# The last matrix of the second layer's weights, converted from float64 beside the attention in memory of its own

## The chip, the cores and the metric

The kernel runs on one core of a Trainium2 chip. The metric is the device time of one execution in microseconds (us). A core has TensorE (PE, matrix products), VectorE (DVE), ScalarE (ACT), GpSimd (POOL) and SyncE (SP, which here issues nearly all loads and stores). Each engine has a queue of its own and works through it in order: an instruction that waits holds back everything behind it on that engine.

## The reference

Three blocks follow each other: an attention over a window of 128 keys, a layer of eight experts of which each token takes one, and a second layer of three products under a maximum. The weights of the second layer are float64 in memory, the others float32.

```python
# q, k, v: [4, 8, 576, 64] float32
scores = np.matmul(q, k.transpose(0, 1, 3, 2)) / 8           # plus a slope for distance, window 128
attn = softmax(scores);  x = (attn @ v) as [2304, 512]
...
logits = x @ w_gate + modality_bias[modality_id]             # 8 experts
h = np.maximum(x[mask] @ w1[e], 0.0)                         # 512 -> 1024, expert e for its tokens
x[mask] = gate_w[mask, None] * (h @ w2[e])                   # 1024 -> 512
...
h = np.maximum(np.maximum(x @ w1, x @ w2), x @ w3)           # float64, 512 -> 768
out = (h @ w_out).astype(np.float32)                         # float64, 768 -> 512
```

## The kernel before

Every product is made from float16 pieces: each operand is split into a high and a low float16 part, and three products (high by high, high by low, low by high) are added in float32. `PASSES` is that list.

**Order of the work.** The text of the program sets the order on every engine; nothing is reordered. Attention runs in steps of one group of four heads (`Attention.run`). When the first half of the tokens has its routes, the experts' layer of that half (`layer1(0)`, `layer1(1)`) is written between the steps of the attention, so that the two share the engines until the attention ends. What is left of `layer1(1)` then runs alone, then the second layer of the first half (`layer2(0)`), then both layers of the second half (`layer1(2)`, `layer1(3)`, `layer2(1)`).

**The experts' weights** (`Weights`). A piece of 512 KB is loaded into one of three staging tiles `st`, ScalarE writes its high part (L960), VectorE its low part (L969), both into one of four tiles `wt`. `get(n)` runs the high part three pieces ahead and issues loads five pieces ahead.

**The second layer's weights** (`Weights2`). There are 24 matrices of 512 KB: 18 of the three products (`g`, three for each of six blocks m) and six of `w_out` (`wo`). A matrix is loaded into a staging tile `st2` (four of them) and turned into float32 by three integer instructions on VectorE (L1113, L1117, L1122), which write a tile `b64` (five of them). `tick()` puts one of the three into the program. Then `finish()` has ScalarE scale it in place (L1142) and write the high part (L1143), and GpSimd writes the low part (L1144). `settled()` calls `finish()` for a matrix once `AGE` = 2 more ticks have gone by; `tick()` does nothing, and does not count, while too many matrices stand unfinished:

```python
if self.gen is None and (self.done == self.n or len(self.half) > B64 - 2):
    return
self.age += 1
```

**Where the ticks come from.** `layer1` adds up an estimate of TensorE time in `free` after each piece of work and calls `tick()` once for each `TICK` = 0.9 of it, but only once the attention has ended, since the tiles `st2`, `b64`, `g` and `wo` lie in a pool (`m2`) that takes the attention's memory. In `layer2(0)` `inner` calls two or four ticks before each product. `g` goes in the order of its use, `wo` comes last and is needed by `outer` (L1202), which first calls `convert(w.n)`.

Of the kernel before, what the change touches and what calls it, by code (L numbers as in the profile page):

```python
# [40 lines left out]
TICK = 0.9  # L41
# [3 lines left out]
ST2 = 4  # L45
B64 = 5
# [4 lines left out]
def windowed_attention_moe_kernel(  # L51
# [869 lines left out]
    class Weights:  # L921
# [10 lines left out]
        def issue(self, upto):  # L932
            while self.issued < min(upto, self.n):
# [6 lines left out]
                if self.more and self.issued % 7 in (1, 2, 4, 6):  # L940
                    st = self.more.tile([128, 1024], I32, name="st2", tag="st2", bufs=ST2).bitcast(F32)
                else:
                    st = self.pool.tile([128, 1024], F32, name="st", tag="st", bufs=3)
# [31 lines left out]
        def get(self, n):  # L975
            self.low(n + 2)
            self.high(n + 3)
            self.issue(n + (9 if self.more else 5))
# [73 lines left out]
    class Weights2:  # L1052
# [3 lines left out]
        def __init__(self, pool):  # L1056
            self.g = None
            self.wo = pool.tile([128, 2, K2, DM], F16, name="wo", bufs=1)
            self.pool = pool
            self.st = {}  # L1060
            self.n = 4 * K2
# [3 lines left out]

        def issue(self, upto):
            while self.issued < min(upto, self.n):
                n = self.issued
                st = self.pool.tile([128, 1024], I32, name="st2", tag="st2", bufs=ST2)
# [12 lines left out]
                self.st[n] = st  # L1082
                self.issued += 1

        def begin(self):
            g = self.pool.tile([128, 6 * K2 * KD * 128], F16, name="g", tag="g", bufs=1)
            self.g = g.rearrange("p (l i m k c) -> p l i m k c", l=2, i=3, m=K2, k=KD)
# [7 lines left out]
        def tick(self):  # L1095

            if self.gen is None and (self.done == self.n or len(self.half) > B64 - 2):
# [6 lines left out]
        def bits(self):  # L1104
# [7 lines left out]
            b = self.pool.tile([128, 512], I32, name="b64", tag="b64", bufs=B64)  # L1112
# [7 lines left out]
            self.issue(n + ST2)  # L1120
# [12 lines left out]
        def finish(self):  # L1133
            if not self.half:
                return
            n, b, _ = self.half.pop(0)
            if n < 3 * K2:
                m, i = divmod(n, 3)
                dst = [self.g[:, l, i, m].rearrange("p k c -> p (k c)") for l in range(2)]
            else:  # L1140
                dst = [self.wo[:, l, n - 3 * K2] for l in range(2)]
# [6 lines left out]
    def moe2(pool, items, w, hmt, n2=C2, both=False, **kw):  # L1148
# [24 lines left out]
        def inner(*xs):  # L1173
            for m in range(K2):
                w.convert(3 * m + 3)
                run = {}
                for i in range(3):
                    for x in xs:
                        for _ in range(4 if w.done < 3 * (m + 2) else 2):
# [13 lines left out]
        def outer(x, yT, c, idxs, gates):  # L1193
            w.convert(w.n)
            hm = hms[:, x % 2]
            for u in range(n2 // 128):
# [3 lines left out]
                for f in range(K2):  # L1200
                    for wl, xl in PASSES:
                        nc.tensor.matmul(  # L1202
                            out=ps, lhsT=hm[:, xl, f, 128 * u:128 * u + 128],
                            rhs=w.wo[:, wl, f, :], start=(n == 0), stop=(n == 3 * K2 - 1),
# [111 lines left out]
    with tc.manual_schedule():  # L1316
# [30 lines left out]
        yT = [big.tile([128, 2, KD, WY], F16, name="yT0", bufs=1)]  # L1347
        xa_cm = tc.tile_pool(name="xa", bufs=1)
# [4 lines left out]
        bats, w2s, m2 = [], None, None  # L1353
# [15 lines left out]
        def settle():  # L1369

            nonlocal w2s, m2, xh
# [3 lines left out]
            w2s = Weights2(m2)  # L1375
# [45 lines left out]
        def layer1(u):  # L1421
            nonlocal acc, free
            i = 0
            for c, dv in moe(mw, wst, u, xT[u], yT[u // 2], wait):
# [15 lines left out]
                if w2s:  # L1440
                    if not w2s.g:
                        w2s.begin()
# [78 lines left out]
```

## Time and profile before

| | us |
|---|---|
| median of 3 runs | 693.69 |
| lowest and highest run | 693.31 and 697.92 |
| the profiled execution, its own time | 690.42 |
| its span (first to last instruction) | 688.6 |
| TensorE busy / VectorE / ScalarE / GpSimd | 642.8 / 364.4 / 347.0 / 225.2 |

Times in the rows below are counted from the span's start. In names the buffer's number is left out, so that `st` stands for the experts' staging tiles and for the second layer's `st2`, and `b` for `b64`; `in_moe_w_dram` stands for the weights of both layers. A matmul's end is modelled, so that the number of matmuls in a stretch says more than TensorE's busy time.

### The profile page before, as it was taken

What the parts mean: (1) busy time and instruction counts of PE and PEld (TensorE: products, weight loads), DVE (VectorE), ACT (ScalarE), POOL (GpSimd) and SP (SyncE); (2) the same over time, 40 slices, a digit from 0 to 9 for tenths busy, and PEclk for the clock granted to TensorE, in tenths of its full rate; (3) what the DMA queues carried; (4) which work ended last, traced back from release to release, by engine and by line L of the source; (5) the groups of instructions that cost most, each with busy time, mean ns of one, the idle gap of its engine ahead of it and who ended that gap; (6) DMA issues with size and microseconds to landing.
All of it is one profiled execution on the core that took longest, in us unless ns stands there. A gap on an engine that the chain in (4) does not pass through costs nothing.

```text
span 688.6 us, 12881 instructions
## 1 busy us (share of the span) xinstructions
PE 642.8 (93%) x4787; PEld 399.7 (58%) x4787; DVE 364.4 (53%) x1083; ACT 347.0 (50%) x660; POOL 225.2 (33%) x232
## 2 busy tenths in 40 slices
PE   6899889989989997899899999999999999999993
PEld 5687755666657545755564564444448666656641
DVE  5977875865567599999922223152224455201100
ACT  5898887887757365854423211454647211111110
POOL 2111226343112255756534212472424111121121
PEclk9999999999999999999999999999999999999997
DMA  9655773455312665674323403343330000000011
GB/s 192 109 124 134 192 202 82 119 148 152 96 47 66 206 202 163 210 245 161 106 60 82 93 17 123 122 141 104 100 115 2 1 0 1 1 32 17 1 46 49
DMA packets 120800, 69.95 MB, mean 102 GB/s; under 512 B 68872, under 2 KB 115484, under 8 KB 120732
## 3 DMA queue, kind: packets, MB, share of 16 engines
q1 hardware_dynamic: 116992, 59.06, 32.2%
q0 software_dynamic: 3040, 9.96, 4.5%
q8 instruction: 40, 0.66, 0.4%
q14 instruction: 28, 0.23, 0.1%
q10 hardware_dynamic: 700, 0.04, 0.1%
HBM read 57.19 MB, written 9.44 MB: 97 GB/s over the span
## 4 chain that ended last, share of the span: by engine, by line
PE 70%; DVE 15%; ACT 8%; issue 3%; DMA 2%; POOL 1%; POOLq 0%; DVEq 0%; ACTq 0%; SPq 0%
PE m L1159 28%; PE m L1018 10%; PE m L997 10%; PE m L1202 9%; PE s L338 3%; PE m L471 2%; DVE wt L969 2%; PE m L379 2%; PE m L286 2%; ACT e L360 2%; DVE b L1117 2%; DVE e L351 2%; DVE b L1113 2%; PE bank L409 2%; ACT eh L385 1%
## 5 line engine op out<-in xcount | busy, mean ns | idle before, releaser
L1159 PEld LDWEIGHTS <-g 128*128 128x128 f16 x1296 | 126.7, 98 | 87.6 <-issue 4.3
L1159 PE MATMUL m<-yT,g 128*128 128x384 f16 x648 | 106.8, 326 | 2.5 <-DVE hx L1168 1.5
L969 DVE SCALAR_TENSOR_TENSOR wt<-st,wt 128x1024 f16<-128x1024 f32 x48 | 64.3, 1341 | 79.3 <-ACT wt L960 79.3
L1159 PE MATMUL m<-yh,g 128*128 128x384 f16 x648 | 105.7, 327 | 0.0
L1018 PE MATMUL m<-ht,wt 128*128 128x496 f16 (+3 forms) x576 | 102.3, 334 | 3.0 <-DVE wt L969 3.0
L1168 DVE SCALAR_TENSOR_TENSOR hx<-m,hx 128x384 f32<-128x384 f32 x72 | 39.7, 555 | 123.5 <-PE m L1159 120.9
L997 PEld LDWEIGHTS <-wt 128*128 128x128 f16 x576 | 55.8, 100 | 49.8 <-DVE wt L969 4.9
L989 POOL TENSOR_TENSOR ht<-hf,ht 128x496 f16<-128x496 f32 (+3 forms) x48 | 51.0, 1068 | 88.5 <-ACT ht L988 82.8
L1018 PEld LDWEIGHTS <-wt 128*128 128x128 f16 x576 | 54.1, 98 | 43.1 <-DVE wt L969 3.7
L360 ACT ACTIVATE e<-e,nm 128x256 f32<-128x256 f32 (+2 forms) x144 | 59.2, 471 | 27.4 <-DVE nm L351 27.0
L987 ACT ACTIVATE hf<-m 128x496 f32<-128x496 f32 (+3 forms) x72 | 35.9, 498 | 64.7 <-PE m L1018 31.9
L997 PE MATMUL m<-xT,wt 128*128 128x496 f16 (+2 forms) x288 | 59.5, 353 | 6.0 <-DVE wt L969 3.9
L997 PE MATMUL m<-xh,wt 128*128 128x496 f16 (+1 forms) x288 | 51.2, 330 | 0.0
L351 DVE CUSTOM_DVE_ANT_0 e<-s,bias 128x256 f32<-128x256 f32 (+1 forms) x128 | 45.8, 381 | 10.1 <-ACT e L360 4.8
L960 ACT ACTIVATE wt<-st 128x1024 f16<-128x1024 f32 x48 | 49.9, 1044 | 1.0 <-DMA st<-in_moe_w_dram 0.9
L390 DVE TENSOR_TENSOR el<-m,eh 128x512 f16<-128x512 f32 x64 | 42.2, 681 | 9.6 <-ACT eh L385 9.6
L1188 POOL TENSOR_TENSOR xh<-hx,xh 128x384 f16<-128x384 f32 x18 | 16.5, 914 | 89.8 <-ACT xh L1187 89.8
L338 PE MATMUL s<-kT,qT 64*128 64x256 f32 (+2 forms) x320 | 42.4, 386 | 3.3 <-DVE nm L351 2.2
L1187 ACT ACTIVATE xh<-hx 128x384 f16<-128x384 f32 x18 | 9.4, 523 | 71.1 <-DVE hx L1168 67.1
L314 POOL TENSOR_TENSOR vl<-rawv,vh 128x512 f16<-128x512 f32 (+1 forms) x20 | 22.5, 1125 | 65.2 <-ACT vh L307 65.2
L1208 ACT ACTIVATE ob<-m,gate 128x512 f32<-128x512 f32 x18 | 12.4, 687 | 55.0 <-PE m L1202 49.6
L385 ACT ACTIVATE eh<-m 128x512 f16<-128x512 f32 x64 | 34.7, 586 | 4.9 <-PE m L379 4.7
(184 smaller groups left out, 987.4 us busy)
## 6 DMA issues: line engine op xcount, KB each, us to landing
st<-in_moe_w_dram SPq DMA_DIRECT2D x66, 512.0 KB, 3.9
rawk<-in_k_dram SPq DMA_DIRECT2D x16, 256.0 KB, 4.3
rawq<-in_q_dram SPq DMA_DIRECT2D x16, 256.0 KB, 4.8
rawv<-in_v_dram SPq DMA_DIRECT2D x16, 256.0 KB, 4.0
xs<-x SPq DMA_DIRECT2D x16, 256.0 KB, 2.2
st<-in_moe_w_out_dram SPq DMA_DIRECT2D x6, 512.0 KB, 3.4
rawk<-in_k_dram SPq DMA_DIRECT2D x4, 128.0 KB, 5.5
rawq<-in_q_dram SPq DMA_DIRECT2D x4, 128.0 KB, 3.7
```

The source lines that it names most:

```text
L338: nc.tensor.matmul(out=out[u][rows, x // 2, c0:c1], lhsT=self.qT[b, t][r, i, 0:n], rhs=self.kT[b][r, i, k0 + c0:k0 + c1], start=True, stop ...
L351: nc.vector.tensor_tensor_reduce(out=e[:, x, c0:c1], in0=s[x % 2][:, x // 2, c0:c1], in1=bias[:, x, c0:c1], scale=-0.125, scalar=3.0e38, o ...
L360: nc.scalar.activation(out=e[:, x, c0:c1], in_=e[:, x, c0:c1], func=ACTF.Exp, scale=-1.0, bias=nm[:, x:x + 1],)
L385: nc.scalar.activation(out=b, in_=a, func=ACTF.Copy)
L390: nc.vector.tensor_tensor(out=o, in0=a, in1=b, op=ALU.subtract)
L960: nc.scalar.activation(out=wt[:, 0], in_=st, func=ACTF.Copy, scale=SW)
L969: nc.vector.scalar_tensor_tensor(out=wt[:, 1], in0=st.rearrange("p (a b) -> p a b", a=a), scalar=SW, in1=wt[:, 0], op0=ALU.mult, op1=ALU.s ...
L989: nc.gpsimd.tensor_tensor(out=lo, in0=hf, in1=hi[1], op=ALU.subtract)
L997: nc.tensor.matmul(out=ps, lhsT=wt[:, wl, kk, o:o + 128], rhs=xT[:, xl, kk, bass.ds(d[0], cap)], start=(n == 0), stop=(n == 3 * KD - 1),)
L1018: nc.tensor.matmul(out=ps, lhsT=wt[:, wl, f, :], rhs=hs[f][:, xl], start=(n == 0), stop=(n == 3 * KF - 1),)
L1159: nc.tensor.matmul(out=ps, lhsT=w.g[:, wl, i, m, kk, :], rhs=yT[:, xl, kk, c:c + n2], start=(n == 0), stop=(n == 3 * KD - 1),)
L1202: nc.tensor.matmul(out=ps, lhsT=hm[:, xl, f, 128 * u:128 * u + 128], rhs=w.wo[:, wl, f, :], start=(n == 0), stop=(n == 3 * K2 - 1),)
```

## The change

`Weights2` is made before the attention ends and gets a pool of its own (`wp`) for the six tiles of `wo`, for two staging tiles `st2` and for two tiles `b64`. The list `order` puts the six matrices of `w_out` first (`EARLY` = 6), then the 18 of `g`. During the attention `layer1` issues loads and ticks for these six, at `SHARE` = 0.3 of the rate. Once the attention has ended, `begin` opens rings of three `st2m` and three `b64m` in `m2` for the 18 others. `tick()` now returns while an unfinished matrix stands in `half` (during the attention), or while two do (after it). `issue(EARLY + ST2)` is called once the attention has ended. The staging tiles of the experts' weights of the second half change too (every second one in `st2m`, eight pieces ahead).

```diff
-ST2 = 4
-B64 = 5
+ST2 = 3
+EARLY = 6
+SHARE = 0.3
...
-                if self.more and self.issued % 7 in (1, 2, 4, 6):
-                    st = self.more.tile([128, 1024], I32, name="st2", tag="st2", bufs=ST2).bitcast(F32)
+                if self.more and self.issued % 2:
+                    st = self.more.tile([128, 1024], I32, name="st2m", tag="st2m", bufs=ST2).bitcast(F32)
...
-            self.issue(n + (9 if self.more else 5))
+            self.issue(n + (8 if self.more else 5))
...
-            self.g = None
-            self.wo = pool.tile([128, 2, K2, DM], F16, name="wo", bufs=1)
+            self.g = self.more = None
+            self.wo = [pool.tile([128, 2, DM], F16, name=f"wo{f}", bufs=1) for f in range(K2)]
...
+            self.order = [3 * K2 + f for f in range(EARLY)] + list(range(3 * K2))
+            self.order += [3 * K2 + f for f in range(EARLY, K2)]
...
+        def ring(self, x, nm, width):
+            if x < EARLY:
+                return self.pool.tile([128, width], I32, name=nm, tag=nm, bufs=2)
+            return self.more.tile([128, width], I32, name=nm + "m", tag=nm + "m", bufs=ST2)
+
         def issue(self, upto):
-            while self.issued < min(upto, self.n):
-                n = self.issued
-                st = self.pool.tile([128, 1024], I32, name="st2", tag="st2", bufs=ST2)
+            while self.issued < min(upto, self.n if self.more else EARLY):
+                n = self.order[self.issued]
+                st = self.ring(self.issued, "st2", 1024)
...
-            if self.gen is None and (self.done == self.n or len(self.half) > B64 - 2):
+            left = (self.n if self.more else EARLY) - self.done
+            if self.gen is None and (not left or len(self.half) > (1 if self.more else 0)):
                 return
...
-            b = self.pool.tile([128, 512], I32, name="b64", tag="b64", bufs=B64)
+            b = self.ring(n, "b64", 512)
...
-            self.issue(n + ST2)
+            self.issue(n + (ST2 if n >= EARLY else 2))
...
-                w.convert(3 * m + 3)
+                w.convert(EARLY + 3 * m + 3)
...
-                        for _ in range(4 if w.done < 3 * (m + 2) else 2):
+                        for _ in range(4 if w.done < EARLY + 3 * (m + 2) else 2):
...
+        wp = ctx.enter_context(tc.tile_pool(name="wp", bufs=1))
+        w2s = Weights2(wp)
...
-                if w2s:
-                    if not w2s.g:
-                        w2s.begin()
-                    w2s.issue(ST2)
-                    if w2s.done == w2s.n:
-                        wst.more = m2
-                    free += c - dv
-                    w2s.settled()
-                    while free > TICK:
-                        free -= TICK
-                        w2s.tick()
+                if m2 and not w2s.more:
+                    w2s.begin(m2)
+                w2s.issue(EARLY + ST2 if m2 else 2)
+                if w2s.done == w2s.n:
+                    wst.more = m2
+                free += (c - dv) * (1.0 if m2 else SHARE)
+                w2s.settled()
+                while free > TICK:
+                    free -= TICK
+                    w2s.tick()
```

Three places show what moves. The first is VectorE's queue just after the attention, at the first two matrices that are converted there; `r_` and `slot_` are routing of the second half, `wt` an expert's piece. Before:

```order
L1122 SCALAR_TENSOR_TENSOR b64_3996<-st2_3976,b64_3996 128x512
L1113 TENSOR_SCALAR b64_4026<-st2_3978 128x512 [waits DMAHW0_49]
L701 TENSOR_SCALAR r_pi_4014<-r_pi_4014 128x5
L702 TENSOR_SCALAR r_pi_4014<-r_pi_4014 128x5
L756 TENSOR_REDUCE r_mn2_3685<-r_le2_3684 1x1 [waits DVE_49]
L705 CAST r_pq_4042<-r_pi_4014 128x2x5 [waits DVE_49]
L758 SCALAR_TENSOR_TENSOR r_sd2_3682<-r_sd2_3682,r_mn2_3685 1x1 [waits DVE_49]
L710 TENSOR_TENSOR r_op_4045<-iota_r_78,r_pq_4042 128x640 [waits DVE_49]
```

After:

```order
L1134 SCALAR_TENSOR_TENSOR b64_4006<-st2_1941,b64_4006 128x512
L1125 TENSOR_SCALAR b64_4051<-st2_3992 128x512 [waits DMAHW1_49,Pool_49]
L702 TENSOR_SCALAR r_pi_4036<-r_pi_4036 128x5
L703 TENSOR_SCALAR r_pi_4036<-r_pi_4036 128x5
L757 TENSOR_REDUCE r_mn2_3702<-r_le2_3701 1x1 [waits DVE_49]
L706 CAST r_pq_4067<-r_pi_4036 128x2x5 [waits DVE_49]
L759 SCALAR_TENSOR_TENSOR r_sd2_3699<-r_sd2_3699,r_mn2_3702 1x1 [waits DVE_49]
L711 TENSOR_TENSOR r_op_4070<-iota_r_78,r_pq_4067 128x640 [waits DVE_49]
```

The matrix that starts here has a wait for GpSimd (Pool) that it didn't have: its tile `b64` is that of the matrix two before it, and GpSimd reads that last.

The second is SyncE's queue at the same time; `st2` and `st2m` are loads of the second layer's matrices, `st` those of the experts. Before:

```order
L1073 DMA st2_3978<-in_moe2_w2_dram 128x4x256 [waits DMAHW0_49]
L1073 DMA st2_3980<-in_moe2_w3_dram 128x4x256
L1073 DMA st2_3982<-in_moe2_w1_dram 128x4x256 [waits DMAHW2_49]
L951 ISA
L951 DMA st_3987<-in_moe_w2_dram 128x8x128 [waits DVE_49]
```

After:

```order
L1089 DMA st2_3994<-in_moe2_w_out_dram 128x1024 [waits DMAHW2_49,DVE_49]
L1089 DMA st2_3996<-in_moe2_w_out_dram 128x1024 [waits DMAHW3_49,DMAHW1_49,DVE_49]
L1089 DMA st2_3998<-in_moe2_w_out_dram 128x1024 [waits DMAHW4_49,DMAHW2_49,DVE_49]
L1083 DMA st2m_4000<-in_moe2_w1_dram 128x4x256 [waits DMASW5_49,DMASW6_49,DMASW4_49,DMASW7_49,DMASW1_49,DMAHW5_49,DMASW0_49,DMAHW6_49,PE_49,DMAHW7_49,Activation_49,Pool_49]
L1083 DMA st2m_4002<-in_moe2_w2_dram 128x4x256
L1083 DMA st2m_4004<-in_moe2_w3_dram 128x4x256
L952 ISA
L952 DMA st_4011<-in_moe_w2_dram 128x8x128 [waits DMAHW0_49]
```

The expert's piece (`st_3987`, now `st_4011`) stands behind three loads that wait for VectorE, each for the last of the three instructions on the matrix two before it.

The third is ScalarE's queue at the pieces and matrices that follow. Before:

```order
L1142 ACTIVATE b64_4026<-b64_4026 128x512 [waits DVE_49]
L1143 ACTIVATE g_3975<-b64_4026 128x512 [waits Activation_49]
L960 ACTIVATE wt_4121<-st_3987 128x1024 [waits DMAHW3_49]
L987 ACTIVATE hf_4159<-m_4125 128x480 [waits PE_49,Pool_49]
L988 ISA
L988 ACTIVATE yT0_749<-hf_4159 128x480 [waits Activation_49]
L1142 ACTIVATE b64_4096<-b64_4096 128x512 [waits DVE_49]
L1143 ACTIVATE g_3975<-b64_4096 128x512 [waits Activation_49]
```

After:

```order
L1155 ACTIVATE b64_4051<-b64_4051 128x512 [waits DVE_49,Pool_49]
L1156 ACTIVATE wo2_755<-b64_4051 128x512 [waits Activation_49]
L961 ACTIVATE wt_4143<-st_4011 128x1024 [waits DMAHW0_49]
L1155 ACTIVATE b64_4113<-b64_4113 128x512 [waits DVE_49,Pool_49]
L1156 ACTIVATE wo3_756<-b64_4113 128x512 [waits Activation_49]
```

The finishing of `b64_4113`, the fourth matrix of `w_out`, now stands directly behind the expert's piece that waits for its load.

## Rows read from the trace of the kernel before

**Rows 1.** Busy time of each engine in two stretches (columns PE, PEld, DVE, ACT, POOL, clock, DMA)

```profile
233.00:342.00 109.00, 99.54 (x655) 61.38 (x654) 104.22 (x169) 65.25 (x115) 64.63 (x53) 0.97 0.62 194
340.00:360.00 20.00, 20.00 (x125) 12.03 (x123) 8.54 (x12) 5.88 (x13) 8.37 (x8) 1.00 0.20 52
```

**Rows 2.** Chain that ended last, by line, from 222 to 300 us

```profile
by line: DVE wt L969 17.0%; DVE b L1117 10.1%; issue 9.7%; DVE b L1122 7.8%; DVE b L1113 7.8%; PE m L1159 6.5%; PE m L1018 5.9%; PE m L997 4.9%; DMA st<-in_moe_w_dram 4.7%; PE m L471 3.3%; DVE r_op L710 2.0%; DVE r_pq L705 1.6%; DVE r_le L7
```

**Rows 3.** Groups on VectorE from 236 to 343 us (count, then busy us, mean ns, idle before)

```profile
L1117 DVE SCALAR_TENSOR_TENSOR b<-st,b 128x512 int32<-128x512 int32 x24 | 25.8, 1075 | 0.4
L1122 DVE SCALAR_TENSOR_TENSOR b<-st,b 128x512 int32<-128x512 int32 x24 | 25.7, 1071 | 0.6
L1113 DVE TENSOR_SCALAR b<-st 128x512 int32<-128x512 int32 x24 | 18.4, 768 | 2.3 <-DMA st<-in_moe_w_dram 2.3
```

**Rows 4.** Timeline of VectorE in the attention (start, us, what, idle before)

```profile
113.32 1.29 DVE L390 TENSOR_TENSOR el<-m,eh 128x512 f16<-128x512 f32 x2 [1.72 <-ACT eh L385]
...
122.76 0.42 DVE L351 CUSTOM_DVE_ANT_0 e<-s,bias 128x256 f32<-128x256 f32 x1
...
135.24 0.68 DVE L390 TENSOR_TENSOR el<-m,eh 128x512 f16<-128x512 f32 x1
```

**Rows 5.** Timeline of VectorE just after the attention

```profile
233.05 1.20 DVE L969 SCALAR_TENSOR_TENSOR wt<-st,wt 128x1024 f16<-128x1024 f32 x1
236.58 0.68 DVE L1113 TENSOR_SCALAR b<-st 128x512 int32<-128x512 int32 x1 [2.33 <-DMA st<-in_moe_w_dram]
237.30 0.69 DVE L1117 SCALAR_TENSOR_TENSOR b<-st,b 128x512 int32<-128x512 int32 x1
...
239.51 0.41 DVE L1113 TENSOR_SCALAR b<-st 128x512 int32<-128x512 int32 x1
...
246.34 0.20 DVE L729 TENSOR_TENSOR r_rhs<-r_ot,parts 128x40 f16<-128x40 f16 x1
...
253.95 1.23 DVE L969 SCALAR_TENSOR_TENSOR wt<-st,wt 128x1024 f16<-128x1024 f32 x1
```

**Rows 6.** Timeline of ScalarE there

```profile
241.25 0.60 ACT L988 ACTIVATE ht<-hf 128x480 f16<-128x480 f32 x1
...
245.78 0.63 ACT L1143 ACTIVATE g<-b 128x512 f16<-128x512 f32 x1
...
255.43 1.04 ACT L960 ACTIVATE wt<-st 128x1024 f16<-128x1024 f32 x1
```

**Rows 7.** Timeline of GpSimd there

```profile
241.93 1.10 POOL L989 TENSOR_TENSOR ht<-hf,ht 128x480 f16<-128x480 f32 x1 [1.02 <-ACT ht L988]
...
246.54 1.34 POOL L1144 TENSOR_TENSOR g<-b,g 128x512 f16<-128x512 f32 x1 [0.88 <-DVE r_rhs L729]
```

**Rows 8.** Timeline of TensorE there

```profile
248.01 14.74 PE L1018 MATMUL m<-ht,wt 128*128 128x480 f16 x72
```

**Rows 9.** Timeline of SyncE's issues there

```profile
229.74 0.39 SPq L951 DMA_DIRECT2D st<-in_moe_w_dram  x1
232.82 2.03 SPq L1073 DMA_DIRECT2D st<-in_moe_w_dram  x4
235.05 9.47 SPq L951 DMA_DIRECT2D st<-in_moe_w_dram  x2
```

**Rows 10.** Busy time in two stretches of 2 us; DMA share and GB/s stand last

```profile
240.00:242.00 2.00, 2.00 (x11) 0.96 (x10) 2.00 (x7) 1.54 (x3) 0.98 (x2) 1.00 0.89 268
242.00:244.00 2.00, 2.00 (x11) 0.98 (x10) 2.00 (x5) 0.89 (x2) 1.02 (x1) 1.00 0.08 24
```

**Rows 11.** From issue to landing, all loads into the tiles `st` and `st2`

```profile
DMA to landing us min/median/max: 3.3/3.9/6.9
```

**Rows 12.** Busy time at the start of the second layer, as in Rows 1

```profile
295.00:324.00 29.00, 29.00 (x179) 17.48 (x179) 27.55 (x34) 14.25 (x27) 16.92 (x15) 1.00 0.64 201
324.00:334.00 10.00, 7.78 (x46) 4.26 (x45) 9.83 (x13) 4.92 (x9) 5.08 (x5) 1.00 0.62 184
```

**Rows 13.** Timeline of TensorE at the first products with `w_out`

```profile
371.72 4.48 PE L1202 MATMUL m<-wo,yh 128*128 128x512 f16 x20 [1.05 <-POOL wo L1144]
```

More of the change, by code (lines that the diff above doesn't have):

```diff
@@ L1081, in issue, with begin @@
                     )
-                self.st[n] = st
+                self.st[self.issued] = st
                 self.issued += 1
-        def begin(self):
-            g = self.pool.tile([128, 6 * K2 * KD * 128], F16, name="g", tag="g", bufs=1)
+        def begin(self, pool):
+            self.more = pool
+            g = pool.tile([128, 6 * K2 * KD * 128], F16, name="g", tag="g", bufs=1)
             self.g = g.rearrange("p (l i m k c) -> p l i m k c", l=2, i=3, m=K2, k=KD)
@@ L1136, in finish @@
             n, b, _ = self.half.pop(0)
+            n = self.order[n]
             if n < 3 * K2:
@@ L1140, in finish @@
             else:
-                dst = [self.wo[:, l, n - 3 * K2] for l in range(2)]
+                dst = [self.wo[n - 3 * K2][:, l] for l in range(2)]
             nc.scalar.activation(out=b, in_=b, func=ACTF.Copy, scale=SW)
@@ L1203, in outer @@
                             out=ps, lhsT=hm[:, xl, f, 128 * u:128 * u + 128],
-                            rhs=w.wo[:, wl, f, :], start=(n == 0), stop=(n == 3 * K2 - 1),
+                            rhs=w.wo[f][:, wl, :], start=(n == 0), stop=(n == 3 * K2 - 1),
                         )
@@ L1352, in windowed_attention_moe_kernel @@
         last = 9 * B + 4
-        bats, w2s, m2 = [], None, None
+        bats, m2 = [], None
         def step():
@@ L1369, in settle @@
         def settle():
-            nonlocal w2s, m2, xh
+            nonlocal m2, xh
             assert next(steps, None) is None
@@ L1374, in settle @@
             m2 = ctx.enter_context(tc.tile_pool(name="m2", bufs=1, side="right"))
-            w2s = Weights2(m2)
             xh = m2.tile([128, 2 * KD * WH], F16, name="xh", tag="xh", bufs=1)
@@ L1468, in windowed_attention_moe_kernel @@
         free_ht = True
-        if not w2s.g:
-            w2s.begin()
+        if not w2s.more:
+            w2s.begin(m2)
         xa_cm.__exit__(None, None, None)
```

## Prediction

> **What bounds the kernel now.** I read the busy time by stretches first, to see which engine is full where. From the end of the attention at 233 us to 342 us VectorE is busy for 104 of 109 us; in the stretch from 340 to 360 it is busy for 8.5 of 20 [rows 1]. The chain that ended last says the same: from 222 to 300 us it runs through VectorE's weight pieces (L969) and the three conversion lines, and only some 17% of it are products [rows 2]. So in these 109 us the time is what VectorE's queue takes, and every idle us of VectorE there is lost unless something later gives it back. After 342 us TensorE is the bound. All 24 matrices are converted in exactly that stretch, three rows each with means of 0.77, 1.08 and 1.07 us [rows 3]; one that runs alone takes 0.41 or 0.69 [rows 5]. The question is therefore how much VectorE work leaves the stretch, and whether the queue still runs without idling.
>
> **What the change moves.** The order of instructions answers the first half: only one of the six matrices of `w_out` is converted beside the attention. After its three instructions it stands in `half`; the new limit makes `tick()` return while anything stands there, and a tick that returns doesn't count. `settled()` wants two more ticks, so nothing is finished until the attention has ended and the limit rises to two. Three VectorE instructions and two loads move; 23 matrices stay.
>
> **In the attention.** The three instructions stand ahead of three rows of VectorE's timeline [rows 4]. The first stands ahead of a row before which VectorE idled 1.72 us for ScalarE, and 0.41 us fits in there: nothing. The second and third stand in busy stretches, ahead of a score row and of a low part: they cost up to their mean lengths, 1.08 + 1.07 = 2.1 us, and if later waits of VectorE swallow them, nothing. Half of that is the value: I take **+1.0**, bounds 0 and +2.1. The two loads go out behind stores of the attention, and the matrices of q, k and v behind them are loaded several groups ahead, so I cost them at nothing; without that cover it would be one landing, 3.9 us [rows 11], once.
>
> **The first new wait.** Before, VectorE waited 2.33 us for the first matrix [rows 5]; now that matrix has long landed, so VectorE starts at 233.05 and would reach the first instruction of the matrix after next at 237.2: before, it took 239.51 - 236.58 = 2.9 us from one matrix's first instruction to the next one's, and the expert's piece of 1.20 now lies between them. There it now waits for GpSimd, because only two tiles `b64` exist and GpSimd must first have read the matrix from the attention. That matrix is finished only now: ScalarE takes it behind `ht`, which ends at 241.25 + 0.60 = 241.85, and needs two rows of 0.63 [rows 6], to 243.1; GpSimd's row of 1.34 [rows 7] follows, to 244.4. So VectorE idles some 7 us. Before, the instruction of this place started at 239.51 and `r_rhs` ended at 246.54, 7.0 us later [rows 5]. The same rows from 244.4 end at 251.4; where GpSimd doesn't stretch the conversion rows (0.41 and 0.69 twice in place of their means, 1.1 us less) at 250.3; I take 250.8, **4.3 us late**. TensorE went on behind `r_rhs` at 248.01 [rows 8] and so now waits some 3 us.
>
> **The second new wait.** SyncE issues in order. The last load of `w_out` waits for the third instruction on the fourth matrix, which follows `r_rhs` after three conversion rows: 1.8 us at the shortest, 2.9 at the means, so at 252.1 to 254.3, and I take 253.1. Behind it stand three loads of `g` and only then the expert's piece. Before, five such loads went out back to back from 232.82 on [rows 9], and the DMA engines were busy until 241.8 (0.89 of the stretch to 242, then 0.08) [rows 10]: 9.0 us from the first issue to the fifth landing, which is also 235.05 + 6.9 [rows 9, 11]. So the piece lands at 262.1. ScalarE makes its high part (1.04, rows 6) by 263.1 and only then finishes the fourth matrix of `w_out` (2 by 0.63), 264.4; GpSimd takes 1.34, 265.7. VectorE stands waiting for that with the sixth matrix, whose `b64` it is, then needs 0.41 for it and 1.20 for the piece: 267.3. Before, this row ended at 253.95 + 1.23 = 255.2 [rows 5]. VectorE is **12.1 us late** there, the first wait included. TensorE needs the piece after 48 of the 72 products that began at 248.01 [rows 8], some 10 us of work after 251, and waits from 261 to 267; since VectorE is the bound, this wait is beside the delay and not on top of it. The bounds: with the usual landing of 3.9 us for the fifth load [rows 11], issued 2.2 us behind the first [rows 9], it is 8.2; with the longer conversion rows all along it is 13.4. I take 12.1, since the five loads in a row are the nearer row.
>
> The page "DMA: Bandwidth & Descriptors" of the Trainium skill gives, in the section on the anatomy of one DMA, a fit of 2.0 us plus the bytes over 436 GB/s; it was fitted on DMAs that GpSimd issues. For five loads of 512 KB that makes an estimate of 8.0 us in place of the 9.0 of the rows, and the forecast would be 1.0 us lower, at 702.2. The rows stand for the same loads on the same queue, so the sum goes by them.
>
> **From there to the second layer** the order on VectorE has the same 16 conversion rows between this piece and the last expert's piece before the second layer, so the delay goes through unchanged. The rings of three `b64m` add waits for GpSimd, but the matrix they wait for is three back, some 8 us, while ScalarE and GpSimd need under 3: nothing, and if that cover is gone it is the last rival below.
>
> **In the second layer** VectorE has four conversion rows fewer to go (38 instead of 41 after the first products' routing, and one before), some 3.9 us. What that gives is bounded by what TensorE lost: 179 products in 29 us are 0.162 us each, so 46 products in the next 10 us [rows 12] are 7.45 us of work, 2.55 lost. I take **-2.6**; if only half of it comes back, -1.3. At the first products with `w_out` TensorE waited 1.05 us for the last matrix's low part [rows 13]; it is now done long before: **-1.0**. The last matrix of `g` takes its place, and its finishing has two products of the next block (3.9 us) in front of it. In the second half TensorE has no waits for weights before, and the ring there gets one tile less; I cost that at nothing, and a piece that came late would cost part of a landing of 3.9.
>
> **The sum**: 1.0 + 12.1 - 2.6 - 1.0 = +9.5 us. Against the profiled execution's own 690.42 us (span 688.6, 1.8 around it) that is 699.9. That execution is 3.3 us under the median of the runs, 693.69, so I forecast **703.2** for the median. The bounds together: 0 + 8.2 - 2.6 - 1.0 = +4.6, or 698.3; and 2.1 + 13.4 - 1.3 - 1.0 = +13.2, or 706.9.
>
> **The rivals.** *The second wait is hidden.* If the expert's piece landed before VectorE comes to it at about 256, only the first wait would stay: 4.3 + 1.0 - 2.6 - 1.0 = +1.7, or **695.4**. It decides from the landing: the fifth of five loads would have to land within 3 us. The busy DMA engines until 241.8 speak against it [rows 10]; for it speaks that I don't see which of the five landed when.
>
> *VectorE doesn't wait at all*, the one that is not slower. If GpSimd gives the tile of the attention's matrix back before 237, VectorE runs on from 233.05: the 2.33 us of rows 5 are gone, the third matrix's load goes out early, and 1.0 - 2.3 - 2.6 - 1.0 = -4.9 gives **688.8**. That needs ScalarE to finish that matrix 6 us earlier than its place behind `ht` allows [rows 6], so little speaks for it.
>
> *The rings bite in the second layer.* If GpSimd gives a `b64m` back later than three matrices after (8.7 us at the mean rows), TensorE's 2.6 us of loss come back and as much again: 9.5 + 5.2 = +14.7, or **708.4**. GpSimd is busy for 64.6 of 109 us [rows 1], which leaves it time; the gathers it also issues there speak for it.
>
> *All six matrices beside the attention*, as the change says, would be another time, but the order has one.
>
> **How the numbers follow.** Chances: the forecast 0.65, the hidden second wait 0.15, no wait 0.08, the rings 0.12. One per cent, 6.9 us, is about what a measurement of this kernel can tell from no change: 686.8 and 700.6 are the edges. Of the forecast's own range, 698.3 to 706.9, about five sixths lie above 700.6. Slower: 0.54 + 0.12 = 0.66. Within 1%: 0.11 + 0.15 + 0.04 = 0.30. Faster: 0.04, the part of the no-wait case that gains more. The range from 695.5 to 707.0 leaves out the no-wait case (0.08), a third of the hidden wait (0.05) and half of the rings (0.07).
>
> **What would show it.** Right: three conversion rows before 233 us; a VectorE row released by GpSimd's `wo` after some 7 us of idling near 244, and another with 8 to 9 us near 266; on SyncE a load of `w_out` waiting for VectorE, with the expert's piece behind it; TensorE waiting for `wt` near 261; no loss around the place of rows 12, moved by some 12 us, and no wait of L1202 for `wo`. Wrong: VectorE without idling after the attention, or a stretch before 233 us that is longer by more than 2 us.

## The result

The median after the change is 704.84 us (702.97 to 707.22, four runs) against 694.9 us of the kernel before on the same chip (its three runs from above and a fourth): a ratio of 1.0144, interval 1.0105 to 1.0184. The forecast was 703.2 us and slower. The profiled execution's span grew from 688.6 to 701.2 us.

Four marks in the trace cut the span into pieces: the last routing row of the attention on VectorE (L482, now L483), the first product of the second layer (L1159, now L1172), the first product with `w_out` (L1202, now L1215), and the end. The pieces, here and in the table of the experiments, are those of one profiled execution each, which can lie some us off the median of its kernel.

| us | attention, to its last routing row | first layer, to the second's first product | second layer, to its first product with `w_out` | the rest |
|---|---|---|---|---|
| before | 232.7 | 60.3 | 73.9 | 321.8 |
| after | 234.8 | 72.1 | 73.8 | 320.5 |
| difference | +2.1 | +11.8 | 0.0 | -1.3 |

**The two waits are there.** First VectorE's timeline after the attention, which answers to [rows 5] (start, us, what, idle before and what ended it):

```profile
235.48 1.21 DVE L970 SCALAR_TENSOR_TENSOR wt<-st,wt 128x1024 f16<-128x1024 f32 x1
...
239.12 0.67 DVE L1134 SCALAR_TENSOR_TENSOR b<-st,b 128x512 int32<-128x512 int32 x1
246.39 0.43 DVE L1125 TENSOR_SCALAR b<-st 128x512 int32<-128x512 int32 x1 [6.59 <-POOL wo L1157]
...
253.20 0.20 DVE L730 TENSOR_TENSOR r_rhs<-r_ot,parts 128x40 f16<-128x40 f16 x1
...
268.72 1.30 DVE L1125 TENSOR_SCALAR b<-st 128x512 int32<-128x512 int32 x1 [9.37 <-POOL wo L1157]
269.94 1.21 DVE L970 SCALAR_TENSOR_TENSOR wt<-st,wt 128x1024 f16<-128x1024 f32 x1
```

VectorE idles 6.59 and 9.37 us, both times for GpSimd's low part of a `wo`. `r_rhs` comes 6.9 us later than in [rows 5], the expert's low part (the last row) ends 16.0 us later than the last row there. ScalarE, GpSimd and SyncE show why, in that order (they answer to [rows 6, 7, 9]):

```profile
243.34 0.60 ACT L989 ACTIVATE ht<-hf 128x480 f16<-128x480 f32 x1
243.85 0.61 ACT L1155 ACTIVATE b<-b 128x512 f32<-128x512 f32 x1
244.49 0.63 ACT L1156 ACTIVATE wo<-b 128x512 f16<-128x512 f32 x1
...
265.22 1.06 ACT L961 ACTIVATE wt<-st 128x1024 f16<-128x1024 f32 x1 [10.76 <-DMA st<-in_moe_w_dram]
266.18 0.61 ACT L1155 ACTIVATE b<-b 128x512 f32<-128x512 f32 x1
266.83 0.63 ACT L1156 ACTIVATE wo<-b 128x512 f16<-128x512 f32 x1
```

```profile
245.20 1.16 POOL L1157 TENSOR_TENSOR wo<-b,wo 128x512 f16<-128x512 f32 x1
...
267.53 1.16 POOL L1157 TENSOR_TENSOR wo<-b,wo 128x512 f16<-128x512 f32 x1 [11.33 <-ACT wo L1156]
```

```profile
232.26 23.29 SPq L1089 DMA_DIRECT2D st<-in_moe_w_out_dram  x4
255.97 1.48 SPq L1083 DMA_DIRECT2D st2m<-in_moe_w_dram  x3
257.65 19.71 SPq L952 DMA_DIRECT2D st<-in_moe_w_dram  x5
```

The matrix from the attention (243.85, 245.20) is finished behind `ht`. SyncE is held by four loads of `w_out` from 232.26 to 255.55; the expert's piece goes out at 257.65, ScalarE can start on it at 265.22, and the finishing of the fourth matrix, for which VectorE waits with the sixth, stands behind it. TensorE's rows answer to [rows 8, 13]:

```profile
253.59 13.32 PE L1019 MATMUL m<-ht,wt 128*128 128x480 f16 x50
271.21 7.12 PE L1019 MATMUL m<-ht,wt 128*128 128x480 f16 x22 [4.30 <-DVE wt L970]
...
380.71 11.82 PE L1215 MATMUL m<-wo,yh 128*128 128x512 f16 x54
```

The wait for `wo` at L1215 is gone. But the loss in the second layer is not; these rows answer to [rows 12], 14 us further on (PE, PEld, DVE, ACT, POOL, clock, DMA share, GB/s):

```profile
309.00:338.00 29.00, 28.82 (x178) 17.37 (x178) 27.51 (x33) 14.35 (x27) 17.43 (x16) 1.00 0.60 193
338.00:348.00 10.00, 8.01 (x48) 4.52 (x47) 9.83 (x13) 4.81 (x9) 4.89 (x5) 1.00 0.69 189
```

### The profile page after: what moved, and what is told of

Its sections match the earlier page's. It is cut to its first block, busy times and chain, and to the rows that moved or that the text cites. A ratio compares the mean times of both kernels' runs of the same rounds, so it can differ in the third digit from the quotient of the medians.

```text
span 701.2 us, 12889 instructions
## 1 busy us (share of the span) xinstructions
PE 646.8 (92%) x4787; PEld 401.5 (57%) x4787; DVE 358.6 (51%) x1083; ACT 346.4 (49%) x660; POOL 225.9 (32%) x232
## 4 chain that ended last, share of the span: by engine, by line
PE 64%; DVE 16%; issue 8%; ACT 7%; POOL 2%; DMA 1%; POOLq 0%; DVEq 0%; ACTq 0%
PE m L1172 25%; PE m L1019 10%; PE m L1215 9%; PE m L998 9%; PE s L339 3%; PE m L380 2%; PE m L287 2%; DVE wt L970 2%; DVE b64m L1129 2%; PE m L472 2%; DVE e L352 2%; DVE b64m L1125 2%; ACT e L361 2%; ACT eh L386 1%; PE bank L410 1%
## 5 line engine op out<-in xcount | busy, mean ns | idle before, releaser
L1172 PEld LDWEIGHTS <-g 128*128 128x128 f16 x1296 | 126.7, 98 | 87.5 <-issue 4.2
L1019 PE MATMUL m<-ht,wt 128*128 128x496 f16 (+3 forms) x576 | 107.9, 346 | 7.0 <-DVE wt L970 7.0
L1172 PE MATMUL m<-yT,g 128*128 128x384 f16 x648 | 106.6, 326 | 2.7 <-DVE hx L1181 1.7
L1172 PE MATMUL m<-yh,g 128*128 128x384 f16 x648 | 105.7, 326 | 0.0
L970 DVE SCALAR_TENSOR_TENSOR wt<-st,wt 128x1024 f16<-128x1024 f32 x38 | 52.5, 1383 | 56.4 <-ACT wt L961 56.4
L998 PE MATMUL m<-xT,wt 128*128 128x496 f16 (+2 forms) x288 | 57.6, 339 | 4.9 <-DVE wt L970 2.9
L961 ACT ACTIVATE wt<-st 128x1024 f16<-128x1024 f32 x38 | 39.5, 1045 | 10.8 <-DMA st<-in_moe_w_dram 10.8
L380 PE MATMUL m<-ident,e 128*128 128x128 f32 (+1 forms) x256 | 36.1, 282 | 1.3 <-issue 0.7
```

The source lines that it names most:

```text
L380: nc.tensor.transpose(ps[:n, x, :], e[:, x, a:z], ident)
L970: nc.vector.scalar_tensor_tensor(out=wt[:, 1], in0=st.rearrange("p (a b) -> p a b", a=a), scalar=SW, in1=wt[:, 0], op0=ALU.mult, op1=ALU.s ...
L998: nc.tensor.matmul(out=ps, lhsT=wt[:, wl, kk, o:o + 128], rhs=xT[:, xl, kk, bass.ds(d[0], cap)], start=(n == 0), stop=(n == 3 * KD - 1),)
L1019: nc.tensor.matmul(out=ps, lhsT=wt[:, wl, f, :], rhs=hs[f][:, xl], start=(n == 0), stop=(n == 3 * KF - 1),)
L1172: nc.tensor.matmul(out=ps, lhsT=w.g[:, wl, i, m, kk, :], rhs=yT[:, xl, kk, c:c + n2], start=(n == 0), stop=(n == 3 * KD - 1),)
```

## The experiments

The theory to test: the loss is (a) VectorE's wait for the tile `b64` of the matrix left unfinished in the attention, and (b) waiting loads of `w_out` in SyncE's queue ahead of an expert's piece. The table has all runs; ratios are to the kernel before on the same chip, with 95% intervals, the columns between are as above.

| run | attention | first layer | second layer | rest | ratio |
|---|---|---|---|---|---|
| after | 234.8 | 72.1 | 73.8 | 320.5 | 1.0144 (1.0105 to 1.0184) |
| e1: short queue | 235.3 | 64.9 | 74.3 | 320.3 | 1.0070 (1.0043 to 1.0097) |
| e5: early finish | 235.5 | 69.5 | 74.1 | 320.5 | 1.0129 (1.0068 to 1.0189) |
| e8: both | 235.4 | 60.9 | 74.3 | 320.4 | 0.9969 (0.9936 to 1.0001) |
| e9: short queue, nothing in the attention | 231.8 | 62.4 | 75.3 | 320.2 | 1.0018 (0.9991 to 1.0045) |
| e10: larger rings | 236.1 | 59.4 | 74.3 | 320.4 | 0.9981 (0.9950 to 1.0012) |
| e6: six in the attention | 244.7 | 60.4 | 70.4 | 320.5 | 1.0016 (0.9994 to 1.0038) |
| e11: six, slower pace | 239.9 | 52.3 | 71.5 | 320.5 | 0.9861 (0.9819 to 0.9903) |
| e15: four, slower pace | 237.7 | 55.7 | 75.4 | 321.4 | 0.9958 (0.9931 to 0.9984) |
| e12: larger rings, slower pace | 239.5 | 54.5 | 78.8 | 320.6 | 1.0006 (0.9978 to 1.0033) |
| e13: before, slower pace | 235.0 | 52.7 | 75.3 | 321.7 | 0.9916 (0.9887 to 0.9945) |
| e16: e11 again | 240.3 | 53.9 | 72.6 | 320.5 | 0.9912 (0.9884 to 0.9940) |
| e17: e13 again | 234.7 | 52.7 | 74.9 | 321.5 | 0.9917 (0.9891 to 0.9944) |

**e1, the queue alone.**

```diff
-w2s.issue(EARLY + ST2 if m2 else 2)
+w2s.issue(min(w2s.done, EARLY) + 2 if m2 else 2)
```

> Medians of the pair so far: before 694.9, changed kernel 704.8. This kernel is the changed one, but after the attention it asks only for loads of w_out whose tile VectorE has already read, so no waiting load stands ahead of the expert's piece; the wait of VectorE for GpSimd near 239 stays. My theory (the piece came late because four loads of w_out held SyncE's queue): of the 13.9 us by which VectorE's low part of that piece came later, 4.8 belong to the first wait and 9.1 to the queue, so VectorE's low part ends near 262 in place of 271 and the time is 704.8 - 9 = 696 (694 to 699). Rival (the two tiles b64, whose finishing stands behind ScalarE's other work, carry the second wait by themselves): 702 to 705, with a wait of 5 us or more for GpSimd's wo left behind the piece. Rival (the DMA engines need the time for those loads wherever they stand): about 701.

Measured: 1.0070, half of the loss gone (the first layer 7.1 us shorter). On 694.9 that is 699.8 us, just over the expected 694 to 699. VectorE's 9.37 us are gone, the 6.83 us for `wo` stay, and two short waits for landings of `w_out`, which is now loaded later, take some 2 us back:

```profile
246.88 0.43 DVE L1125 TENSOR_SCALAR b<-st 128x512 int32<-128x512 int32 x1 [6.83 <-POOL wo L1157]
...
258.07 1.01 DVE L1125 TENSOR_SCALAR b<-st 128x512 int32<-128x512 int32 x1 [0.29 <-DMA st<-in_moe_w_out_dram]
...
262.66 0.43 DVE L1125 TENSOR_SCALAR b<-st 128x512 int32<-128x512 int32 x1 [1.86 <-DMA st<-in_moe_w_out_dram]
```

So the queue is the second wait's cause: no wait for GpSimd is left behind the piece, which the rival with the ring alone asked for.

**e5, the early finish alone.** The age counts on while a matrix waits, and the attention converts one matrix only:

```diff
-left = (self.n if self.more else EARLY) - self.done
+left = (self.n if self.more else 1) - self.done
+self.age += 1
 if self.gen is None and (not left or len(self.half) > (1 if self.more else 0)):
     return
-self.age += 1
```

> The changed kernel with the one early matrix also finished by ScalarE and GpSimd beside the attention; the held queue stays as it is. My theory: VectorE no longer idles 6.6 us near 239, the routing and with it the last load of w_out come 4.8 us earlier, and the rest of the chain follows: 704.8 - 4.8 = 700.0 (698 to 702), with the wait of 9 us near 260 still there. Rival (the second wait ends by something that the first doesn't move, so the gain is eaten there): 704 to 705.

Measured: 1.0129, near the rival (704 to 705 us, 1.013 to 1.015), and the span only 1.6 us shorter; but the interval takes in the expected 5 us and none at all. The trace says where they went:

```profile
240.26 0.41 DVE L1125 TENSOR_SCALAR b<-st 128x512 int32<-128x512 int32 x1
...
250.41 0.43 DVE L1125 TENSOR_SCALAR b<-st 128x512 int32<-128x512 int32 x1 [3.78 <-POOL wo L1157]
...
255.32 0.43 DVE L1125 TENSOR_SCALAR b<-st 128x512 int32<-128x512 int32 x1 [1.05 <-POOL wo L1157]
...
266.72 1.30 DVE L1125 TENSOR_SCALAR b<-st 128x512 int32<-128x512 int32 x1 [9.25 <-POOL wo L1157]
```

The wait near 239 is gone, but the matrices behind it wait 3.78 and 1.05 us on the same ring of two, and the 9.25 us of the held queue follow. I had costed the first wait as if it stood alone.

**e8, both edits.**

> Both edits together: the early matrix is finished beside the attention, and no load of w_out waits in the queue ahead of the expert's piece. My theory (the two waits are the whole loss, apart from 2.1 us in the attention): the second layer began 14 us later in the changed kernel; without the waits that goes, VectorE also saves the 2.3 us that it waited for its first matrix in the kernel before, and the wait for wo at the first products with w_out (1.1 us) stays away: 694.9 + 2.1 - 2.3 - 1.1 = 693.6 (691 to 697). Rival (the new order or the smaller rings cost something by themselves, for instance two tiles b64 in place of five): 698 to 702, with waits of VectorE for GpSimd left in the first layer.

Measured: 0.9969, for an expected 693.6 on 694.9, 0.998. The first layer takes 60.9 us, 60.3 before the change: the held queue and the unfinished matrix together are its whole loss, though VectorE still waits 3.70 and 1.05 us for GpSimd on the ring of two.

**e9, nothing in the attention** (`SHARE = 0.0` beside the edit of e1).

> The changed kernel with no conversion beside the attention at all (share 0) and no waiting load ahead of the expert's piece: only the order of the matrices, the early loads and the rings are left of the change. My theory: the attention ends where it did in the kernel before (2.1 us earlier than in the changed one), VectorE starts on a matrix that has long landed, 694.9 - 2.3 - 1.1 = 691.5, and one more matrix left in the stretch adds up to 2.9: 691 to 695. Rival (the conversion rows beside the attention were free, and the 2.1 us came from somewhere else, as the two early loads): the attention ends 2 us late here too, 694 to 697. Rival (the rings carry a loss): 698 or more.

Measured: 1.0018, no gain, and over the expected 691 to 695 us (0.994 to 1.000). The attention ends at 231.8 us, but this end scatters: in the four traces without a conversion row there (before, e9, e13, e17) it lies between 231.8 and 235.0. The stretch in which the three rows stand is steadier. From the routing row near 110 to that near 179 us it takes 68.2 to 68.7 us in these four, and 69.3 to 70.2 in the six that have the three rows there (the changed kernel, e1, e5, e8, e10 and e12): **+1.5 us** between the means, where 1.8 (0.42 + 0.69 + 0.68) would be the rows' whole length. What e9 doesn't gain is in its first layer: its conversions start there without a finished matrix, and VectorE waits 5.7 us for `wo` on the ring of two.

**e10, larger rings.** From the third matrix on both tiles come from the rings of three in `m2`:

```diff
-            if x < EARLY:
+            if x < 2:
...
-self.issue(n + (ST2 if n >= EARLY else 2))
+self.issue(n + (ST2 if n >= 2 else 2))
...
-w2s.issue(EARLY + ST2 if m2 else 2)
+w2s.issue(2 + ST2 if m2 else 2)
```

> The changed kernel with its one early matrix, where from the third matrix on both tiles (staging and b64) come from the rings of three that hold the attention's former memory, and only loads that need no tile back are asked for at once. Nothing is finished beside the attention. The last run with both waits edited gave 0.997 of the kernel before and still showed VectorE waiting 3.7 and 1.05 us for GpSimd's wo. My theory after these runs (the ring of two b64 is the first wait's cause and takes back most of what the early finish gives): VectorE waits for GpSimd nowhere between 238 and 265, some 4 us less than that run: 0.991 of the kernel before (0.987 to 0.996). Rival (three loads right behind the attention delay the expert's piece, as the five loads did): a wait of VectorE or ScalarE for a landing of 4 us or more and 0.998 to 1.005. Rival (VectorE is the bound, but TensorE's low granted clock in this stretch sets the end): the wait goes and the time stays at 0.997.

Measured: 0.9981. VectorE waits for GpSimd nowhere, as expected, and yet the time is that of e8: my step from idle time to time failed. The first layer in e8, then in e10 (columns as above):

```profile
235.39:296.33 60.94, 53.54 (x376) 34.17 (x376) 54.21 (x114) 39.95 (x69) 36.84 (x27) 0.94 0.61 194
```

```profile
236.05:295.47 59.42, 52.60 (x377) 34.27 (x376) 57.50 (x114) 40.69 (x71) 36.91 (x28) 0.94 0.61 198
```

VectorE idles 4.8 us less (1.9 in place of 6.7) and is busy 3.3 us longer with the same 114 rows: what was a wait became longer rows. So e10 gains 1.5 us net in this stretch, not 4.8, and that from two single traces whose kernels differ in the early finishing too. The time is the one that the rival with TensorE's low clock forecast, but the granted clock is 0.94 in both rows and VectorE is busy for 57.5 of 59.4 us, TensorE for 52.6; with fewer conversion rows for VectorE the stretch gets shorter (e11, e13 below). So VectorE's queue still sets it.

**e6, six matrices in the attention**, as the words of the change say (limit `> 1` throughout, `SHARE = 0.6`, and the edit of e1).

> All six matrices of w_out converted beside the attention, as the words of the change say: the limit in the attention is one matrix in half, the share is 0.6, and no load waits ahead of the expert's piece. The order has 18 conversion rows ahead of the last routing row of the attention, but the same 37 between it and the second layer's first product. My theory (a row beside the attention costs some 0.5 us, since the three rows made the stretch between two routing rows 109 to 178 us longer by 1.5; behind it nothing gets shorter, because the pace of ticks fills the first layer with matrices of g instead): the attention ends 18 x 0.5 = 9 us later, the second layer loses 2.5 us less and wo is there (1.1): 1.008 of the kernel before (1.002 to 1.015). Rival (the rows are hidden beside the attention and leave VectorE's stretch): six matrices of 2.9 us are gone, 0.98 or less.

Measured: 1.0016, below the expected 1.008 and just outside its bounds, and far from the 0.98 of full hiding. The first layer has as many conversion rows as before and takes 60.4 us as before; the second layer is 3.4 us shorter. The end of the attention in this one trace is 12 us later. The start of its second layer, which answers to [rows 12]:

```profile
307.10:336.10 29.00, 29.00 (x180) 17.49 (x179) 26.71 (x34) 14.31 (x27) 17.16 (x16) 1.00 0.46 143
336.10:346.10 10.00, 10.00 (x64) 5.99 (x63) 1.67 (x3) 2.02 (x4) 2.62 (x3) 1.00 0.54 107
```

No loss here. In the program's order VectorE has groups of 2, 2, 2 and 6 conversion rows between its rows of `hx` (before and after: two such rounds, then 2, 2, 2, 5 before and 2, 2, 2, 2 after); here only one round. Before and after, TensorE's waits begin while VectorE works at the second group of six, with VectorE full from the attention on. The group alone isn't the cause: e11 below has two groups of six as well, but VectorE has slack ahead of them (busy for 4.8 of the second layer's first 8 us), and TensorE's one wait there is 0.60 us:

```profile
332.41 30.87 PE L1172 MATMUL m<-yT,g 128*128 128x384 f16 x189 [0.60 <-DVE hx L1181]
```

So what counts is how far VectorE's queue has fallen behind by then; the second group is where it shows.

**e11, six at a slower pace** (`TICK = 1.4` in place of 0.9, `SHARE = 0.9`): 26 conversion rows ahead of the second layer's first row on VectorE in place of 37.

> The same with a slower pace of conversion in the first layer (a tick for 1.4 in place of 0.9 of credit; the share is 0.9, so that the attention still holds all 18 rows): 26 conversion rows in place of 37 between the attention and the second layer. My theory (VectorE's queue is what the first layer takes): 11 rows of 0.98 us are 10.8 us less for VectorE, of which TensorE, which loses 7 us in that stretch, can win at most 7: 0.998 to 1.002 of the kernel before, 4 to 7 us under the run with all six at the old pace. Rival (TensorE's low clock there, not VectorE, sets the stretch): the same time as at the old pace.

Measured: 0.9861, faster than both kernels and than expected. The first layer takes 52.3 us:

```profile
239.90:292.15 52.25, 50.08 (x376) 32.89 (x376) 47.92 (x106) 36.53 (x63) 30.58 (x25) 1.00 0.63 202
```

TensorE is nearly full, at full granted clock. Whether the pace does it or the early matrices, three more kernels tell.

**e13, the kernel before with `TICK = 1.4` alone; e12, e10 with that pace (`SHARE = 0.5`); e15, four matrices in the attention (`EARLY = 4`, `SHARE = 0.5`) with that pace.**

> The kernel before with nothing changed but the pace of conversion in the first layer: a tick for 1.4 in place of 0.9 of credit. The order has 26 conversion rows in place of 37 ahead of the second layer's first row on VectorE, and two bursts of six and four more rows in the second layer. The run with six matrices beside the attention and this pace gave 0.986; this one tells how much of that is the pace. My theory: the first layer takes 52.3 us as in that run in place of 60.3, nothing is paid in the attention (7.2 there), and each burst of six rows more in the second layer costs TensorE 2.3 us, as the second burst does now: 688.6 - 8 + 4.6 = 685, 0.995 (0.989 to 0.999). Rival (the gain came from the early conversion): 1.000 or more. Rival (the bursts are free here): 0.988.

> The changed kernel with one matrix beside the attention, the tiles from the third matrix on from the rings of three, and the slower pace. The order has 33 conversion rows behind the attention ahead of the second layer's first row on VectorE (37 at the old pace; the second layer needs more of them early, since w_out's six come first), then bursts of 7, 6 and 5. My theory: 4 rows fewer make the first layer 3 us shorter than with the rings alone, the larger burst costs TensorE about what it wins: 0.998 of the kernel before, the same as with the rings alone (0.994 to 1.002). Rival (the pace is all): 0.986 to 0.990.

> Four matrices of w_out beside the attention (12 rows; the last two behind all of g), the slower pace, and no load that waits ahead of the expert's piece. My theory: a row beside the attention costs 0.4 us (18 rows cost 7.2 in the best run so far), so 12 cost some 5; the first layer takes 52 us as in that run; the second layer loses 2.3 at its second burst: 232.7 + 5 + 52.3 + 73.9 + 320.8 = 684.7, 0.988 to 0.994 (0.994 if the first layer isn't as short). Rival (the more matrices beside the attention the better): clearly over 0.986 by 4 rows per matrix, 0.995 or more.

Measured: e13 0.9916, within its bounds: the first layer is as short as in e11 with no early conversion at all, and the 11 conversion rows that the second layer has more (a third group of six and one of four among them) cost 1.4 us there, not 4.6. e12 1.0006, within its bounds: with few matrices early, `w_out` ahead of `g` makes the second layer force more conversions, 78.8 us of it. e15 0.9958, over its bounds: its first layer takes 55.7 us in place of the expected 52. VectorE waits 3.72 us for a landing at its start (2.16 in e13), and the granted clock of the stretch is 0.95 (0.97 in e13); how much of the 3 us that is wasn't tested. The time is on the rival's side (0.995 or more), but the next pair speaks against the rival, since six early matrices do no better than none.

**e16 and e17, the two best on one chip.**

> Six matrices beside the attention and the slower pace, the same kernel as in the run that gave 0.986, now on one chip with the kernel before at the slower pace, which gave 0.992 on another: is the early conversion worth anything beyond the pace? My theory: yes, little. Beside the attention its 18 rows cost 4.3 us in the stretch in which most of them stand, the second layer's first products take 71.4 us in place of 75.3 and the wait for wo (1.3) goes, the first layer is as short in both (52.3 and 52.7): 4.3 - 0.4 - 3.9 - 1.3 = 1.3 us under the other, 0.988 to 0.990 of the kernel before and 0.996 to 1.000 of the other. Rival (the difference of 0.986 and 0.992 is real in its size): 0.986 again and 3 to 4 us under the other. Rival (the attention pays for all): the other is faster by 2 us or more.

> The kernel before with the slower pace alone, the partner of the run with six matrices. My theory: 0.991 of the kernel before, as on the other chip (0.989 to 0.994), 1 to 2 us over its partner. Rivals: as there, 3 to 4 us over it, or 2 us under it.

Measured: 0.9912 and 0.9917, medians 684.65 and 684.58 us, so the expected 1.3 us between them isn't there. The 0.986 didn't come again. The early conversion of all six is worth nothing that can be measured beyond the pace: in these two traces, of which e16's is the slowest execution of its kernel, the attention is 5.6 us longer with it, the second layer and the rest 3.3 us shorter. Both beat the two kernels of the change; the simpler one is the kernel before with one number changed.

## Why the prediction was right, step by step

- **VectorE is the bound after the attention** [rows 1 to 3]: right. Two waits of 16.0 us in all on VectorE made the first layer 11.8 us longer (the 37 conversion rows behind the attention, as many as before, took 29.1 us in place of 34.4, which gave a part back), and 11 conversion rows fewer (e13) made it 7.6 us shorter.
- **Only one matrix beside the attention**: right; three rows stand there.
- **The attention, +1.0**: mis-sized within its bounds. The rows cost 1.5 (e9's comparison); the 2.1 of the profiled pair holds scatter of either sign as well. By its letter it meets a sign that the prediction named for being wrong, a stretch before 233 us that is longer by more than 2 us; since that mark scatters by 3 us with no conversion row at all, it decides nothing.
- **The first wait**: right in place (6.59 us for some 7). It made `r_rhs` 6.9 us late, of which 2.1 is the attention, so 4.8 for the 4.3. Not foreseen: removing it alone gives 1.6 of span, since the same ring of two waits again (e5).
- **The second wait**: right in mechanism (e1 removes it). The last load of `w_out` went out some 2 us after the forecast 253.1, which is the attention's delay; from there ScalarE took 10 us to the piece for the 9.0 of the working. The fit of 2.0 us plus bytes over 436 GB/s ("DMA: Bandwidth & Descriptors" of the Trainium skill, anatomy of one DMA), 8.0 us by estimate, is further off than the rows. The low part ended 16.0 us late with the attention, 13.9 without, for 12.1; some 2 us came back before the second layer, so that the first layer's +11.8 meets the term. That it meets it to 0.3 us is partly luck, since the prediction let the delay go through unchanged.
- **The second layer, -2.6**: failed, the one step that did. I took the loss of [rows 12] as one that four fewer of VectorE's rows would lift. It falls at the second group of six rows, and all rows up to there stand in the changed kernel too (73.9 and 73.8 us); the rows saved were at the end, where TensorE lost nothing. e6, where that group is gone, shows 39.00 of 39 us busy.
- **The wait for `wo`, -1.0**: right, -1.3.
- **The sum**: +9.5 was forecast; the medians differ by 9.9, the profiled spans by 12.6 (2.1 + 11.8 + 0.0 - 1.3). Of the 3.1 us between forecast and spans, 2.6 is the failed step and 1.1 the attention; the wait for `wo` and the first layer take 0.6 off. That the median still came within 1.6 us of the forecast is in part luck: the profiled execution lay 4.5 us under the median of the kernel before and 1.9 us under that of the changed one, and this difference hides the failed step. In the chances, five sixths of the range lie above 700.6 only if its middle counts for more; by its width it is under three quarters.
- **The rivals**: a hidden second wait and no wait are excluded by the two rows of VectorE; the rings don't bite in the second layer (73.8 us). All six beside the attention, which I left aside because the order has one, is e6: no change that can be measured.

e6's attention ends 12 us later than before the change and e11's 7, with the same 18 rows. Between the same two routing rows, first e6, then e11:

```profile
185.40:226.69 41.29, 37.65 (x309) 24.34 (x309) 28.39 (x100) 27.89 (x55) 10.27 (x12) 0.88 0.17 55
186.49:221.92 35.43, 32.65 (x309) 21.45 (x309) 28.70 (x100) 27.78 (x55) 10.45 (x12) 1.00 0.21 65
```

The same 309 products take 5.9 us longer at the granted clock of 0.88, more than the whole 4.8 between the two ends; ahead of this stretch e6 isn't behind. So the extra comes with TensorE's lower clock in that execution and not with the rows, which are the same. The scatter of the attention's end has it too: from 178.3 us on, the stretch to the next routing row takes 21.8 us at the granted clock of 1.00 in e9, and from 177.6 us on 23.4 at 0.93 in the kernel before.

What stays open: why the clock was lower there in one execution and not in the other; and what the early loads alone cost in the attention. Not tried: a third `b64` in the pool `wp`.

## What to carry to other kernels

A load that must wait for its tile doesn't only wait: on an engine that issues in order it holds every load behind it, so ask for it no earlier than its tile comes free, or put the urgent loads ahead. Work that is moved early leaves a stretch shorter only if the program's pace there changes too; here the ticks filled the freed places with other matrices, and the pace was the number worth changing. An idle time that is removed is worth what the rows behind it gain, and where two engines slow each other, that can be a part of it (1.5 of 4.8 us from e8 to e10).

## What the runs showed of the hardware

- **Rows stretch when the other engine no longer waits.** From e8 to e10 the 31 conversion rows of VectorE in the first layer went from a mean of 0.76 to 0.83 us as its waits for GpSimd went; the instructions are the same. In both traces, and in those of before, after, e1, e6, e11, e13 and e16, every conversion row behind 200 us that took longer than 0.45 (the first of the three) or 0.72 us (the others) stands beside a GpSimd row; without one beside it no row did. Some rows beside a GpSimd row weren't longer either.
- **TensorE's products were slower behind its long waits.** For the same products of the first layer its busy time was 59.4 us in the changed kernel and 50.1 in e11:

```profile
234.81:306.89 72.08, 59.44 (x376) 35.71 (x376) 53.84 (x113) 40.76 (x71) 36.80 (x29) 0.86 0.52 166
```

The granted clock (the first column behind POOL's) was 0.86 there and 1.00 in e11's row above. Two stretches of the changed kernel, the wait of 4.30 us and the products behind it:

```profile
266.90:271.20 4.30, 0.01 (x1) 0.00 (x0) 2.48 (x3) 4.21 (x8) 2.64 (x3) 0.80 0.08 28
271.20:275.00 3.80, 3.79 (x10) 1.50 (x11) 3.73 (x9) 2.15 (x3) 2.42 (x2) 0.50 0.40 138
```

In the 3.8 us behind the idle time the clock was granted at its lower level, 1.2 GHz, and the 22 products from 271.21 took 7.12 us, 0.32 each, where they took 0.20 in [rows 8]. The prediction had no term for this. Whether any of it reached the time isn't shown: the first layer's +11.8 us is less than VectorE's delay of 13.9.
